# A fused sparse attention and gated FFN kernel: the first FFN unit of three blocks becomes two units of two blocks, fed by 1 KB reads on two DMA queues

## The chip, the cores and the metric

The kernel runs on one core of a Trainium2 chip. A core has five engines with a program each: TensorE (PE: matrix products and transposes into PSUM), VectorE (DVE), ScalarE (ACT), GpSimd (POOL) and SyncE (SP, which here issues DMAs only). They meet at semaphores. Sixteen DMA engines move data between device memory and the on-chip buffer. The metric is device time in microseconds (us) of one launch, the median of three runs.

## The reference

Inputs are q, k and v of shape (4 batches, 8 heads, 768 rows, 64) and three FFN matrices (512 x 1536, 512 x 1536, 1536 x 512), all float32. For each batch and head:

```python
k_min, k_max = min and max of k over chunks of 32 keys          # 24 chunks
ub = sum over d of max(q * k_min, q * k_max)                    # bound of each query on each chunk
top = the 6 chunks of largest ub among those not after the query's own chunk
scores = q @ k.T / 8, kept where the key's chunk is in top and the key is not after the query
attn_out = softmax(scores) @ v
```

The heads are then put side by side, x is (3072, 512), and

```python
out = ((1 / (1 + exp(-(x @ w_gate)))) * (x @ w_val)) @ w_out
```

The first 128 rows of a batch see at most four chunks, so no choice is needed there: they are plain causal attention on the batch's first 128 keys.

## The kernel before

The work is cut into blocks of 128 query rows, six a batch. Three blocks make a **unit** of 384 rows (L659), and a unit goes through two stages: attention of its blocks, then its FFN. There are eight units. A "first" block of a batch (rows 0 to 127) needs only a simple path, `first` (L805); the others need bounds, choice of chunks and masks (`prepare`, L1191: `keys_wide`, `queries_wide`, `choose`), then `attend` (L1047). Unit 0 is made of the first blocks of batches 0, 1 and 2; unit 1 of blocks 1 to 3 of batch 0; unit 2 of blocks 4 and 5 of batch 0 and the first block of batch 3; the rest go on in order.

`load_first` (L731) reads k, q and v of a first block on SP's queue: k and q in two DMAs each (heads 0 to 3, heads 4 to 7), rows of 64 floats, so runs of 256 B (L742), v in one (L737). `first` turns k and q with four f32 TensorE transposes each (L815: `kfT`, `qfT`), copies them to f16 (`kf16`, `qf16`), makes scores (L852), exponentials (L857, ACT), the causal mask (L859, POOL), products with v (L866, `pvf`), divides (L872, L874), turns the result (L881, `xpsf`) and copies it into the unit's x (`xTf`, L885). For batch 0 it also makes minima and maxima of chunks (L825) and the key buffer `hk` (L831).

`ffn` (L1131) runs 12 blocks of 128 hidden columns. For each, four matmuls make the gate product `g` and four the value product `v` (L1146, 128 x 384), ACT takes tanh (L1154), DVE multiplies (L1158, `hg`). Then for each of three row blocks 12 matmuls make the output `o` (L1168), ACT or DVE evicts it (`osb`) and SP stores it (L1180). All FFN products of a unit and of all units are in one order on TensorE (the key "ffn").

The weights come on POOL's queue, converted to f16 on the way, in nine DMAs of 1 MB of f32: three of gate and value columns each (L718, L719), three of output rows (L724). The first pair waits for batch 1's q (L1202), the others for the last causal mask of unit 0 (L1203 to L1208). `load_wide` (L747) reads unit 1's and unit 2's k and q, `load_v` (L771) the values, both on SP.

The order on each engine is not written by hand: every operation is given to a planner (`Plan`, L72) with the engines that can do it, its cost, what it reads and writes, its buffers and a priority. `walk` (L110) places operations one at a time on engines by start time and priority, within limits on buffers (L558), and gives one fixed order for each engine, in which the program is then emitted. The table NUDGES (L304) shifts priorities, and LANDS (L492) holds the planner's landing times of DMAs. So every engine executes in the planned order; what comes late on the chip holds up what stands behind it.

Before the first loads land, POOL and DVE make identities and masks. The eight `hkp` copies (L704) write the mask pattern into the two key buffers.

Of the kernel before, what the change touches and what calls it, by code (L numbers as in the profile page):

```python
# [9 lines left out]
F16 = mybir.dt.float16  # L10
AF = mybir.ActivationFunctionType
ALU = mybir.AluOpType
AX = mybir.AxisListType
# [7 lines left out]
SHARED = {128: (0.145, 0.95), 256: (0.173, 0.90), 512: (0.22, 0.83), 768: (0.29, 0.78), 2048: (0.5, 0.5)}  # L21
SENT, LANDED = {SP: 700, POOL: 2700}, 1100
# [12 lines left out]
class Op:  # L35
    def __init__(self, name, engines, emit, prio, dma, rows, port):
        self.name, self.engines, self.emit, self.prio, self.dma = name, engines, emit, prio, dma
        self.rows, self.port = rows, port
        self.deps = []
        self.bufs = []  # L40
        self.start = self.done = self.engine = None

# [29 lines left out]
class Plan:  # L72
# [37 lines left out]
    def walk(self, land, prio=None, script=None, slow=1.0):  # L110
# [3 lines left out]
        line = {SP: 0.0, POOL: 0.0}  # L114
# [105 lines left out]
        while avail:  # L220
            best = None
            at = {}
            for op in avail:
                r = room(op)
                if r == FAR:
                    continue
                for e in op.engines:
                    at[op, e] = max(r, inputs(op, e))
# [27 lines left out]
    def landings(self, out, slow=1.0):  # L256

        queues = {SP: [], POOL: []}
# [6 lines left out]
        while queues[SP] or queues[POOL]:  # L265
# [5 lines left out]
            if len(on) == 2:  # L271
# [21 lines left out]
    def order(self):  # L293

        nudge = {n: int(x) for n, x in (w.rsplit(":", 1) for w in NUDGES.split())}
        lands = {n: float(x) for n, x in (w.rsplit(":", 1) for w in LANDS.split())}
        prio = {op: op.prio + nudge.get(op.name, 0) * 0.01 for op in self.ops}
# [7 lines left out]
ident:370 epat0:-92 epat:-143 kcr0:-70 kcr1:88 hq0:-119 hq1:74 ap0:168 v10:48 hkp000:102 hkp001:162 hkp010:1  # L305
hkp011:-53 ap1:113 v11:43 hkp100:139 hkp101:127 hkp110:-301 hkp111:-12 ident16:15 kf0_0:-159 kf1_0:-55 qf0_0:-66
qf1_0:-51 vf_0:27 kf0_1:-30 kf1_1:-16 qf0_1:-8 qf1_1:65 vf_1:10 kf0_2:24 kf1_2:41 qf0_2:-23 qf1_2:-11 vf_2:54
k0_u1:-125 k1_u1:-15 k2_u1:-44 k3_u1:35 q0_u1:-10 q1_u1:29 q2_u1:-4 q3_u1:38 v_0_1:-51 v_0_2:-11 v_0_3:24 kfT_0:99
kf16_0:-28 kxf0:60 kxf1:201 kcr_f:18 hkf0:348 hkf1:-115 qfT_0:94 qf16_0:-40 v16_0_0:238 scf_0:-96 expf_0_0:-210
cmf_0_0:18 pvf_0_0:-76 rzf_0_0:194 xf_0_0:-87 xpsf_0_0:190 xTf_0_0:126 expf_0_1:-202 cmf_0_1:-55 pvf_0_1:108  # L310
rzf_0_1:77 xf_0_1:-247 xpsf_0_1:216 xTf_0_1:349 kfT_1:222 kf16_1:-105 qfT_1:-70 qf16_1:-58 vf1_1:10 vc_1:-234
scf_1:49 expf_1_0:-380 cmf_1_0:208 pvf_1_0:-84 rzf_1_0:273 xf_1_0:-212 xpsf_1_0:67 xTf_1_0:-358 expf_1_1:-13
cmf_1_1:373 pvf_1_1:-205 rzf_1_1:48 xf_1_1:-97 xpsf_1_1:-211 xTf_1_1:-218 kfT_2:17 kf16_2:-63 qfT_2:-262 qf16_2:-119
vf1_2:-47 vc_2:-401 scf_2:-119 expf_2_0:66 cmf_2_0:-66 pvf_2_0:255 rzf_2_0:-8 xf_2_0:219 xpsf_2_0:-211 xTf_2_0:202
expf_2_1:-179 cmf_2_1:-80 pvf_2_1:247 rzf_2_1:84 xf_2_1:169 xpsf_2_1:-154 xTf_2_1:59 wv0:48 wg1:-259 wv1:-69 wg2:-2
wv2:1 wo0:-37 wo1:-37 wo2:30 kn_u1_0:121 kT_u1_0:338 kx0_u1_0:215 kx1_u1_0:9 kt_u1_0:-348 hk0_u1_0:-32 hk1_u1_0:-121
kn_u1_1:299 kT_u1_1:179 kx0_u1_1:118 kx1_u1_1:7 kt_u1_1:23 hk0_u1_1:-212 hk1_u1_1:-168 kn_u1_2:314 kT_u1_2:32
kx0_u1_2:84 kx1_u1_2:86 kt_u1_2:100 hk0_u1_2:223 hk1_u1_2:90 kn_u1_3:176 kT_u1_3:-24 kx0_u1_3:385 kx1_u1_3:83
kt_u1_3:-167 hk0_u1_3:64 hk1_u1_3:138 kcr_u1:-25 qn_u1_0:-215 qT_u1_0:68 qf_u1_0:-35 qm_u1_0:223 hq0_u1_0:-426
hq1_u1_0:-4 qn_u1_1:-36 qT_u1_1:84 qf_u1_1:-93 qm_u1_1:3 hq0_u1_1:-255 hq1_u1_1:145 qn_u1_2:20 qT_u1_2:-117  # L320
qf_u1_2:86 qm_u1_2:-137 hq0_u1_2:-331 hq1_u1_2:-54 qn_u1_3:-137 qT_u1_3:-59 qf_u1_3:-21 qm_u1_3:-21 hq0_u1_3:-280
hq1_u1_3:74 ub_u1:37 ubn0_u1:-7 mx0_u1:-11 ap0_u1:130 ubn1_u1:222 ubm1_u1:87 mx1_u1:25 ap1_u1:-112 apt0_u1:-48
hqm0_u1_0:16 hqm0_u1_2:7 apt1_u1:155 hqm1_u1_0:-182 hqm1_u1_2:-99 v16_0_1:177 v16_0_2:318 v16_0_3:471 g_u0_0:36
tanh_u0_0:-46 v_u0_0:-424 hg_u0_0:-188 g_u0_1:-109 tanh_u0_1:-131 v_u0_1:-383 hg_u0_1:-86 g_u0_2:-132 tanh_u0_2:-104
v_u0_2:-243 hg_u0_2:-198 g_u0_3:-77 tanh_u0_3:106 v_u0_3:-80 hg_u0_3:87 g_u0_4:-317 tanh_u0_4:-279 v_u0_4:-282
hg_u0_4:86 g_u0_5:-64 tanh_u0_5:-125 v_u0_5:-235 hg_u0_5:-7 g_u0_6:-14 tanh_u0_6:-83 v_u0_6:-416 hg_u0_6:-27
g_u0_7:-132 tanh_u0_7:54 v_u0_7:-309 hg_u0_7:70 g_u0_8:67 tanh_u0_8:-18 v_u0_8:-445 hg_u0_8:131 g_u0_9:-48
tanh_u0_9:-449 v_u0_9:-447 hg_u0_9:-33 g_u0_10:-62 tanh_u0_10:118 v_u0_10:-430 hg_u0_10:90 g_u0_11:-149
tanh_u0_11:-38 v_u0_11:-294 hg_u0_11:-101 o0_u0_0:267 o1_u0_0:95 o2_u0_0:-2 osb_u0_0:-109 out_u0_0:104 o0_u0_1:371
o1_u0_1:146 o2_u0_1:27 osb_u0_1:34 out_u0_1:315 o0_u0_2:288 o1_u0_2:44 o2_u0_2:258 osb_u0_2:-41 out_u0_2:135  # L330
# [977 lines left out]
```

The softmax here doesn't subtract the row's maximum and nothing guards it: scores larger than these inputs give would overflow.

## Time and profile before

| what | value |
|---|---|
| median of three runs | 295.02 us (294.74 to 295.06) |
| profiled execution | 295.64 us |
| its span, first to last instruction | 293.9 us |
| TensorE busy | 278.2 us |
| mean granted TensorE clock | 0.988 |
| first product of unit 0's FFN starts | 21.61 us |
| first issue of a weight DMA | 10.14 us |

The profile is of one execution. Busy time of an engine leaves out its waits and the issuing of DMAs; PE spans of pipelined matmuls overlap, so the distance between starts is the better price of one. A group of lines in a timeline gives start, length, engine, line of the kernel, operation, output and input, count, and in brackets the idle time ahead of it and what ended it. DMA share is the mean busy share of the sixteen DMA engines; it can exceed 1 where packets of several transfers overlap.

### The profile page before, as it was taken

To read this page: it belongs to the slowest core of one execution; us is meant where nothing else is said; L and a number is where in the kernel's file an instruction comes from. 1 tells how busy PE (TensorE), PEld (TensorE's weight loads), DVE (VectorE), ACT (ScalarE), POOL (GpSimd) and SP (SyncE) were. 2 spreads that over 40 slices of the span, in tenths; PEclk is the share of its full clock that TensorE was granted. 3 is DMA by queue.
4 is the path that set the end of the run, shared out by engine and by line. 5 is a ranking of instruction groups with operands and counts; after the bars stand their busy time and mean duration, and the time that the engine had idled before them with its cause. 6 is when DMAs were issued, how large, how long until landed. Compare 5 with 4: busy or idle time off the path is not lost.

```text
span 293.9 us, 6954 instructions
## 1 busy us (share of the span) xinstructions
PE 278.2 (95%) x2656; PEld 176.7 (60%) x2656; DVE 189.2 (64%) x560; ACT 195.8 (67%) x398; POOL 92.5 (31%) x162
## 2 busy tenths in 40 slices
PE   2879998999989999999999999999999999999994
PEld 2645555767664566556666667676565557655651
DVE  8375883996999289999999899654134124432420
ACT  7674757977984879458889898886563466323321
POOL 6681314933652337013326954213000011000000
PEclk9977999999999999999999999999999999999999
DMA  7999999999967999399997300001100110011002
GB/s 165 218 249 216 197 197 235 220 146 166 184 100 90 203 188 184 67 215 152 142 210 145 111 3 3 0 2 39 71 2 1 50 60 0 2 38 71 0 15 95
DMA packets 123233, 32.69 MB, mean 111 GB/s; under 512 B 111424, under 2 KB 120128, under 8 KB 123200
## 3 DMA queue, kind: packets, MB, share of 16 engines
q1 hardware_dynamic: 118448, 27.53, 53.1%
q0 software_dynamic: 4752, 4.72, 9.5%
q8 instruction: 21, 0.34, 0.5%
q14 instruction: 12, 0.10, 0.1%
HBM read 30.67 MB, written 6.29 MB: 126 GB/s over the span
## 4 chain that ended last, share of the span: by engine, by line
PE 78%; DMA 10%; DVE 4%; SPq 2%; POOL 2%; ACT 1%; issue 1%; ACTq 0%; DVEq 0%
PE o_u L1168 20%; PE v_u L1146 18%; PE g_u L1146 18%; PE sc_u L1063 11%; DMA wo<-in_moe_w_out_dram 9%; PE pv_u L1096 6%; PE ube_u L1002 2%; SPq L742 2%; PE xps_u L1123 2%; DMA qf<-in_q_dram 1%; DVE qf_u L969 1%; DVE kcr L787 1%; DVE kt L953 1%; ACT attf L857 1%; PE qfT L815 1%
## 5 line engine op out<-in xcount | busy, mean ns | idle before, releaser
L1074 ACT ACTIVATE att_u<-sc_u 128x512 f16<-128x512 f32 (+3 forms) x184 | 88.0, 549 | 13.9 <-PE sc_u L1063 13.1
L1158 DVE SCALAR_TENSOR_TENSOR hg_u<-gate_u,v_u 128x384 f16<-128x384 f16 x96 | 51.8, 544 | 53.8 <-PE v_u L1146 37.0
L1146 PE MATMUL g_u<-xT_u,wg 128*128 128x384 f16 x384 | 79.3, 330 | 0.0
L1146 PE MATMUL v_u<-xT_u,wv 128*128 128x384 f16 x384 | 78.8, 328 | 0.3 <-DMA wv<-in_moe_w_val_dram 0.3
L1154 ACT ACTIVATE gate_u<-g_u 128x384 f16<-128x384 f32 x96 | 47.6, 495 | 39.1 <-DVE hg_u L1158 21.5
L1168 PE MATMUL o_u<-wo,hg_u 128*128 128x512 f16 x288 | 68.0, 379 | 1.1 <-DMA wo<-in_moe_w_out_dram 1.1
L1080 POOL TENSOR_SCALAR_AFFINE_SELECT att_u<-att_u 128x384 f16<-128x384 f16 (+1 forms) x56 | 28.4, 512 | 99.0 <-ACT att_u L1074 98.2
L1146 PEld LDWEIGHTS <-wv 128*128 128x128 f16 x384 | 36.8, 98 | 23.5 <-issue 0.8
L1146 PEld LDWEIGHTS <-wg 128*128 128x128 f16 x384 | 36.5, 99 | 21.8 <-issue 1.5
L1168 PEld LDWEIGHTS <-hg_u 128*128 128x128 f16 x288 | 27.1, 98 | 28.7 <-issue 1.5
L1177 ACT ACTIVATE osb_u<-o_u 128x512 f32<-128x512 f32 x20 | 12.1, 603 | 26.7 <-PE o_u L1168 25.0
L1096 PEld LDWEIGHTS <-att_u 128*128 128x128 f16 x640 | 25.5, 98 | 4.7
L1096 PE MATMUL pv_u<-v,att_u 128*128 128x65 f16 x640 | 28.0, 193 | 0.0
L1063 PE MATMUL sc_u<-hqo,hko 128*128 128x128 f16 (+2 forms) x220 | 27.8, 243 | 0.1
L1063 PE MATMUL sc_u<-hqe,hke 128*128 128x128 f16 (+2 forms) x220 | 27.1, 243 | 0.2 <-ACT att_u L1074 0.2
L1063 PEld LDWEIGHTS <-hke 128*128 128x128 f16 x220 | 16.8, 98 | 5.7 <-issue 1.2
L779 POOL CAST v<-v 128x512 f16<-128x512 f32 x23 | 13.9, 619 | 19.2 <-DMA v<-in_v_dram 18.9
L1063 PEld LDWEIGHTS <-hko 128*128 128x128 f16 x220 | 16.3, 98 | 4.8 <-issue 0.2
L576 DVE COPY xT_u<-xps_u 128x384 f16<-128x384 f16 (+1 forms) x17 | 5.7, 338 | 14.4 <-PE xps_u L1123 14.3
L1115 DVE TENSOR_TENSOR x_u<-pv_u,rz_u 128x384 f16<-128x384 f32 (+1 forms) x28 | 14.5, 523 | 0.4
L1025 DVE MAX8 mx_u<-ubn_u 128x8 f32<-128x8 f32 (+16 forms) x152 | 12.4, 156 | 0.1
L787 DVE TRANSPOSE_TENSOR_REDUCE kcr<-k 128x24 f32<-128x768 f32 x12 | 11.2, 941 | 0.8 <-DMA k<-in_k_dram 0.8
(119 smaller groups left out, 306.9 us busy)
## 6 DMA issues: line engine op xcount, KB each, us to landing
out_dram<-osb_u SPq DMA_DIRECT2D x24, 256.0 KB, 2.4
v<-in_v_dram SPq DMA_DIRECT2D x23, 256.0 KB, 5.0
k<-in_k_dram SPq DMA_DIRECT2D x12, 384.0 KB, 6.1
q<-in_q_dram SPq DMA_DIRECT2D x12, 384.0 KB, 6.8
wg<-in_moe_w_gate_dram POOLq DMA_DIRECT2D x3, 512.0 KB, 10.2
wv<-in_moe_w_val_dram POOLq DMA_DIRECT2D x3, 512.0 KB, 12.8
wo<-in_moe_w_out_dram POOLq DMA_DIRECT2D x3, 512.0 KB, 23.3
kf<-in_k_dram SPq DMA_DIRECT2D x8, 128.0 KB, 3.6
```

The source lines that it names most:

```text
L779: plan.add(f"v16_{b}_{ib}", {POOL: pool(H * D)}, lambda e: nc.gpsimd.tensor_copy(v16[b % 2][:, ib, :, 0:D], at(t)), reads=[t], writes=[("v ...
L787: plan.add(f"kx{m}_{name}_{p}", {DVE: dve(size)}, lambda e, m=m, op=op: nc.vector.tensor_reduce(out=outs[m](), in_=src(), op=op, axis=AX.X ...
L1025: nc.vector.max(at(mx)[:, e_, j, :], at(ubn)[:, e_, j, 0:max(8, u.seen[j])])
L1063: nc.tensor.matmul(at(t)[:, o:o + 128 * m], hk[b % 2][e_][:, p, 128 * jb:128 * jb + 128], hq[u.side][e_][:, p, 128 * x:128 * (x + m)], sta ...
L1074: plan.add(f"exp_{u.name}_{h}_{y}", {ACT: act(n)}, lambda e, t=t, att=att, b0=b0, n=n: nc.scalar.activation(at(att)[:, b0:b0 + n], at(t), ...
L1080: nc.gpsimd.affine_select(out=dv, in_=dv, compare_op=ALU.is_ge, fill=0.0, base=0, pattern=[[0, u.m], [1, 128]], channel_multiplier=-1)
L1096: nc.tensor.matmul(at(pv)[:, last, x, :], at(att)[:, c:c + 128], v16[b % 2][:, jb, h, :], start=(jb == 0), stop=(jb == ib))
L1115: plan.add(f"x_{u.name}_{p}", {DVE: dve(u.t)}, lambda e: nc.vector.tensor_tensor(at(x_).rearrange("p a (e d) -> p e a d", e=2), at(pv)[:, ...
L1146: nc.tensor.matmul(at(t), w16[:, c, 128 * fb:128 * fb + 128], at(u.xt)[:, c, :], start=(c == 0), stop=(c == 3))
L1154: plan.add(f"tanh_{u.name}_{fb}", {ACT: act(T)}, lambda e, g=g, gate=gate: nc.scalar.activation(at(gate), at(g), AF.Tanh, scale=0.5), read ...
L1158: plan.add(f"hg_{u.name}_{fb}", {DVE: dve(T)}, lambda e, w_=w_, gate=gate, hg=hg: nc.vector.scalar_tensor_tensor(at(hg), at(gate), 1.0, at ...
L1168: nc.tensor.matmul(at(o), at(hgs[fc])[:, 128 * tb:128 * tb + 128], wo16[:, fc, :], start=(fc == 0), stop=(fc == NFB - 1))
```

## The change

Unit 0 keeps the first blocks of batches 0 and 1 (256 rows). A new unit 8 has the first blocks of batches 2 and 3, and unit 2 is left with its two other blocks (256 rows). All sizes that were T = 384 in `ffn` follow the unit's rows. Unit 8's products form an order of their own ("ffn8") beside the others, and both small units make four gate products ahead of the first value product.

```diff
     units = [
-        Unit(0, [], [(0, 0), (1, 1), (2, 2)]),
+        Unit(0, [], [(0, 0), (1, 1)]),
         Unit(1, [(0, 1), (0, 2), (0, 3)]),
-        Unit(2, [(0, 4), (0, 5)], [(3, 2)]),
+        Unit(2, [(0, 4), (0, 5)]),
...
+        Unit(8, [], [(2, 0), (3, 1)]),
     ]
```

First blocks are read with four consecutive rows a partition (1 KB runs), k on SP's queue and q on ACT's; v alternates between the two. Since a partition then holds four rows, k and q are turned by eight f32 matmuls against the identity instead of four transposes, and the f16 copy puts the rows in order.

```diff
-                for e_ in range(2):
-                    plan.add(f"{n}f{e_}_{b}", {SP: (450, 450)}, lambda e, t=t[n], src=src, e_=e_: nc.sync.dma_start(
-                        at(t).rearrange("s (p e) d -> s e p d", e=2)[:, e_], heads(src, b, e_)[:, 0:128].rearrange("p s d -> s p d")),
...
+                for g in range(2):
+                    plan.add(f"{n}f{g}_{b}", {(SP, ACT)[j]: (450, 450)}, lambda e, view=view, src=src, g=g: issue(e).dma_start(
+                        view()[:, 256 * g:256 * g + 256], heads(src, b, g)[:, 0:128].rearrange("p (s r) d -> p s (r d)", r=4)),
...
             def turn(e, t=t, n=n):
-                for p in range(NP):
-                    nc.tensor.transpose(at(t)[:, p], at(raw[n])[:, 2 * p:2 * p + 2].rearrange("s e d -> s (e d)"), ident32)
...
+                for r in range(4):
+                    for g in range(2):
+                        c = 256 * g + 64 * r
+                        nc.tensor.matmul(at(t)[ROWS[g], r].rearrange("d p s -> d (p s)"), raw[n][0]()[:, c:c + 64], ident32,
+                                         start=True, stop=True)
```

The first pair of weight loads waits for batch 1's k. All weight loads are chained by the order of their issues, no longer by the last causal mask.

```diff
-    weights(0, -0.9, [(raw_f[1]["q"], 1)])
-    last = next(op for op in plan.ops if op.name == "cmf_2_1")
...
+    gate = [raw_f[1]["k"][1][1]]
+    weights(0, 4, -15.0, gate)
+    weights(4, 8, -1.6, [])
+    weights(8, 12, -1.6, [])
```

37 f32 matmuls of the identity with itself, whose result nobody reads, are put on TensorE: eight at the start, the others each not before a named step of a first block starts.

```diff
+    warm = ps("warm", "wm", [128, 128])
+    for name, n in {"": 8, "kfT_0": 2, "qfT_0": 3, "kfT_1": 3, "qfT_1": 3, "scf_1": 3, "kfT_2": 3, "qfT_2": 3, "scf_2": 3, "pvf_2_0": 3}.items():
+        for i in range(n):
+            op = plan.add(f"warm{name}_{i}", pe(213, 170), lambda e: nc.tensor.matmul(at(warm), ident32, ident32, start=True, stop=True),
+                          reads=["ident32"], writes=[warm], prio=5.0)
+            wake.append((op, name))
```

Buffers: the f16 keys, queries, values and attention weights of the first blocks are lent parts of batch 1's key and value buffers (and of `hq`) through a new class `Lent`; what writes those buffers later waits for the first blocks' last use. The bounds' transposed copy `ubn` shares the buffer of `qm`, whose next writer comes after it (`held`). There are three x buffers instead of two, 21 of `hg` instead of 18, and six of `np` instead of seven. The first four `hkp` copies come after unit 8's first gate product, the other four after unit 1's.

The planner knows a third queue (ACT) and a new table of packet prices, an operation can be given an earliest start (table HOLDS), and NUDGES and LANDS have new values throughout, so the order on every engine is planned anew.

## The prediction

> **What bounds the kernel now.** First the page: busy shares, then the strip of 40 slices (7.35 us each).
> ```profile
> PE 278.2 (95%) x2656; PEld 176.7 (60%) x2656; DVE 189.2 (64%) x560; ACT 195.8 (67%) x398; POOL 92.5 (31%) x162
> ...
> PE   2879998999989999999999999999999999999994
> ...
> PEclk9977999999999999999999999999999999999999
> DMA  7999999999967999399997300001100110011002
> ```
> TensorE is the bound almost everywhere, and only the first seven slices (to 51 us) show anything to recover: PE at 2, 8, 7, a clock of 7 tenths in slices 3 and 4, and DMA engines that are full from slice 2 on. So I cut the span into stretches (busy us of each engine, count, granted clock, DMA share, GB/s):
> ```profile
> 0.00:21.60 21.60, 12.61 (x93) 9.16 (x94) 14.08 (x38) 15.21 (x25) 14.97 (x30) 0.93 1.09 210
> 21.60:48.10 26.50, 25.05 (x178) 14.44 (x176) 17.70 (x60) 16.68 (x39) 6.62 (x13) 0.93 1.19 211
> 48.10:62.40 14.30, 13.99 (x189) 9.88 (x190) 12.46 (x43) 11.86 (x32) 8.81 (x20) 1.00 1.00 202
> 62.40:289.00 226.60, 225.53 (x2199) 142.97 (x2200) 144.94 (x422) 151.50 (x304) 62.07 (x101) 1.00 0.51 85
> ```
> From 48.1 us PE is idle 0.31 + 1.07 us in 241 us. Whatever makes the kernel faster must get more TensorE work done before 48 us or remove such work. The waits of PE before 65 us (us in total, times, longest) and its timeline where the first products start say how the early time goes:
> ```profile
> PE kfT L815 <- DMA kf<-in_k_dram: 5.9, 2, 5.0
> PE pvf L866 <- POOL attf L859: 1.2, 2, 1.1
> PE o_u L1168 <- DMA wo<-in_moe_w_out_dram: 1.1, 1, 1.1
> ```
> ```profile
> 19.82 0.42 PE L881 MATMUL xpsf<-ident,xf 128*128 128x128 f16 x2
> 20.91 0.90 PE L901 MATMUL kT_u<-ident,kn_u 128*128 128x128 f32 x3 [0.67 <-ACT kn_u L574]
> 21.61 1.49 PE L1146 MATMUL g_u<-xT_u,wg 128*128 128x384 f16 x4
> 22.89 1.49 PE L1146 MATMUL v_u<-xT_u,wv 128*128 128x384 f16 x4
> 24.17 1.38 PE L1146 MATMUL g_u<-xT_u,wg 128*128 128x384 f16 x4
> 25.39 0.81 PE L1146 MATMUL v_u<-xT_u,wv 128*128 128x384 f16 x4
> 26.04 0.81 PE L1146 MATMUL g_u<-xT_u,wg 128*128 128x384 f16 x4
> ```
> Start to start a product of four matmuls is 1.28 us at first, 0.65 us from 25.39 on: three products lose 0.63 + 0.63 + 0.57 = 1.83 us to the halved clock. And the products cannot start before 20.6 us, since the third block's x is turned only at 19.82 (copied out at 20.28 + 0.29). Last, the chain that ended last runs through the weight stream, not through PE:
> ```profile
> 7.48 3.85 DMA qf<-in_q_dram
> ...
> 22.11 25.94 DMA wo<-in_moe_w_out_dram
> 48.09 1.89 PE o_u L1168 x8
> ```
> The weights land (issue time plus time to landing) at 18.3, 22.2, 27.3, 31.2, 34.6, 38.0, 41.4, 44.7 and 48.05 us, 3.7 us apart on average; PE filled nearly all of that time with other work.
>
> **What the Trainium skill says.** "TensorE: Matmul & The Clock Gate", Part 1: the array runs at 1.2 GHz until about 3.4 us of activity and at 2.4 GHz after. The trace agrees: 1.28 against 0.65 us. "DMA: Bandwidth & Descriptors", Specifications: runs under 512 B fall below line rate; same page, Issuing engines are not separate DMA queues: a second queue only saves issue time. The trace agrees as far as it goes: SP issues one load per 0.55 us and the engines move 124 GB/s in the first 5 us, 210 afterwards with 256 B runs; no 1 KB run is in it. "TensorEngine Tiling (Array Packing)", Restrictions: column tiling switches the fast FP32 transpose off. The trace has both forms: a turned block of four is 0.44 to 0.47 us (60.17, 60.64, 61.08), and the column-tiled f32 bounds (L1002, 320 columns, eight tiles side by side) take 36.47 to 37.03, so 0.56 us, 0.22 us for 128 columns.
>
> **The ledger before.** I count useful TensorE work at full-clock prices. One first block costs, in the saturated stretch where the block of batch 3 runs, 0.47 + 0.44 (turns) + 0.33 (scores) + 0.14 + 0.13 (values) + 0.23 (x turned) = 1.74 us. Up to 21.6: three blocks 5.2, three key turns of unit 1 at 0.33, so 6.2 us. From 21.6 to 48.1: 26.5 - 1.45 idle - 1.83 cold = 23.2. Done by 48.1: 29.4 us.
>
> **The change, part by part.**
> (1) *Loads.* Twelve k and q loads of batches 0 to 2 go from 256 B to 1 KB runs, four for batch 3 come forward from 50.9 us, with its v. At 210 GB/s 128 KB took 0.6 us. The 1 KB price is not shown: no gain 0.6, at best the page's fabric ceiling 0.3; I take 0.4. Sixteen at 0.4 plus a v of 1.2 instead of twelve at 0.6 is 7.6 against 7.2 us: no DMA time is saved before 48 us, it is only used sooner. SP and ACT issue together, so k and q of batches 0 and 1 (1 MB) land at about 6.2 us (first issue 0.81, 1.4 us to data, 4 us of transfer), where batch 1's q came at 10.1. A load moved to ACT occupies it for about 0.5 us: ten of them, 5 us, take the place of two 1.47 us constant copies (3.09, 4.58), which move.
> (2) *Weights* are gated by batch 1's k instead of its q: first issue 10.14 to about 6.3. They then share with 2 MB of first blocks still to come, so I give half of it back: 2 us earlier, first gate weights at 16.5, last output weights at 46 (at most 3.8, at least 0).
> (3) *Turns.* Eight turns of plain f32 matmuls in place of eight transposes. Four pairs at 0.22 us are 0.9 if the two column halves run side by side (as L1002's tiles do), 1.8 if not; I take 1.0. The extra 0.55 x 8 = 4.4 us lies in the first 17 us, where PE was idle for 9 us of 21.6, so it costs nothing; without that cover it is 2.2 us for the two blocks ahead of the first product.
> (4) *Two units of 256 rows.* Unit 0 needs two blocks only. Batch 1's x is ready 7 us after its q in the trace (qfT 10.18 to xT 16.80 + 0.37); 6.2 + 7 + 2 x 0.55 and 1 us of ACT issue gives about 15.3. So the first product starts with the weights, S = 17 (15.5 to 21). Unit 8 follows about 6 us later. Split products: 384 columns are 162.5 ns, 128 are 55, so 256 are 109; three units of 24 x 4 x 109 = 31.4 against two at 31.2: +0.2 us. Evictions: 36 at about 0.37 (ACT) and 0.42 (DVE) against 24 at 0.49 and 0.54: +1.6 and +2.2 us, mostly at 21.6 to 48.1 us, where ACT has 9.8 and DVE 8.8 us free, and batch 3's own evictions leave 55 to 69 us; 0.
> (5) *Batch 3's block* leaves the saturated stretch; in the ledger it counts as work done early.
> (6) *Warming matmuls*, 37 f32 ones of 0.22 us: ahead of S in idle time they cost nothing and save the 1.83 us of cold clock. Those after S stand in PE's fixed order ahead of real products; some five in the way: 1.1 us (0 to 3).
> (7) *Moved constants and shared buffers.* Eight mask copies (0.5 us each on DVE) leave 3 to 8 us: four come after unit 8's first product, four after unit 1's, at 64 to 80 us, where DVE is 85% and ACT 98% busy and PE waited 0.8 us for DVE once: 0.3 us (0 to 1.5). The bounds' transposed copy sharing the queries' buffer makes the next unit's positive part wait; before, the copies were read by 40.9 and the next queries come at 50: 0. The borrowed key and value buffers are free long before batch 1's keys: 0.
>
> **The sum.** By S = 17 two blocks (3.5) and the turns of the other two (1.8) are done: 5.3. From 17 to 48.1 are 31.1 us, less 1.1 for (6) and 0.3 of cold clock, less waits. Waits: between gate and value weights (3.5 us apart) only 1.7 us of gate products and some 0.6 of block work are ready: 1.2 idle. To the second gate weights 5 us hold 1.7 of value products, 3.5 of unit 8 if its x is there by 23, and 1.4 of other work: about 1. Later each quarter brings 7 us of products per 7 us of stream and the last output wait of 1.12 us goes. Scattered waits, as many as before: 1. So 5.3 + 31.1 - 1.1 - 0.3 - 3.2 = 31.8 us done against 29.4: 2.4 us gained. After 48.1 (4) and (7) take some 0.4. Net 2.0. The tail (last eviction and store, 4 us) is unchanged. What is late next is the weight stream: it sets S and the 3.2 us of waits.
> The profiled execution is 295.64 us (span 293.9 and 1.74 around it): 293.6 after. The median shown is 0.62 lower, 295.02: so **293.0 us**.
>
> **Rivals.** *A, the stream only moves the wait* (0.16): the DMA engines are already full, the extra batch and the earlier start cancel, S is 19 to 20 and PE waits in 20 to 36 us. Against it: PE has unit 8's 7 us of products in hand. Gain 2.0 - 2.5 + 0.5 of smaller waits: 295.0.
> *B, ACT as an issuer is late* (0.16). ACT runs in order; behind its ten loads are the casts of k and q, the exponentials and x copies of the four blocks, and PE waits for each. SP's issues of first blocks rose from 0.5 to 0.99 us when its queue was backed up (5.86): ten such are 10 us instead of 5. It decides when unit 0's x comes later than the first value weights (about 20 us). At S = 21.5 the 2.4 us of gain lose 4.5, get back 2.0 of the waits for weights (landed by then), lose 0.8 to a late x of unit 8 and the 0.4 after 48 us: 1.3 us slower than before, 296.3; with a cold start too, 297.5.
> *C, more than that* (0.08): weights 3.8 us earlier, S = 15.5, no waits after 25: 290.7.
> That the change does nothing is excluded: a third of the early products change size and place.
>
> **Chances.** The forecast has 0.60, with its own range 291.4 to 294.4. 0.2% (0.6 us) is about what a measurement of this kernel can tell from no change. Faster: nearly all of 0.60, C, and a little of A: 0.67. Same: 0.11 (most of A). Slower: 0.22 (B and the bad end of A). Range for 8 in 10: 291.0 to 296.6.
>
> **What would show it.** Right: first product near 17 us with PEclk full to 26 us; unit 8's products by 24; first wg issue near 6.3; no wait for wo; no kfT or qfT after 24 us; PE idle under 2 us after 48. Wrong: ACT's issues over 0.8 us, S beyond 20, turns at 1.8 us, or DVE the releaser of PE at 64 to 85 us.

## The result, and the profile after

The changed kernel takes 317.14 us (median; 316.12 to 317.45) where the kernel before takes 295.04 (294.74 to 295.08): a ratio of 1.0746 [1.0720, 1.0771]. The prediction said 293.0 us, with 291.0 to 296.6 around it. It was wrong in sign and by more than ten times the size. An execution more than 1.5% above the fastest of its kernel counts as slow and is left out of every ratio below; this concerns two of the seven executions of one version, the hold on batch 1's queries.

Beside the strip shown of before, these are the same rows of the page after (40 slices of 7.88 us):
```profile
PE 289.3 (92%) x2916; PEld 199.9 (63%) x2916; DVE 193.9 (61%) x574; ACT 191.7 (61%) x401; POOL 100.2 (32%) x169
...
PE   4242799999999999999999999999999999999995
...
ACT  0002677749879783879489678977767663363321
...
PEclk9555599999999999999999999999999999999999
DMA  2935899995984999997890089201100010001002
```
All of the loss is in the first five slices. PE is idle for most of 30 us, ACT does nothing at all before the fourth slice, and the DMA engines, which were full from the second slice on before, are at 3 and 5 tenths in slices 3 and 4. From the sixth slice on PE is as full as ever. The cut into stretches says when (busy us of each engine, granted clock, DMA share, GB/s):
```profile
0.00:5.00 5.00, 3.41 (x16) 3.22 (x16) 2.38 (x8) 0.00 (x0) 3.22 (x13) 1.00 0.13 37
...
15.00:20.00 5.00, 1.97 (x16) 1.57 (x16) 0.00 (x0) 0.00 (x0) 0.00 (x0) 0.50 0.53 120
20.00:25.00 5.00, 1.98 (x16) 1.58 (x16) 0.00 (x0) 0.00 (x0) 0.00 (x0) 0.50 0.42 102
25.00:30.00 5.00, 1.22 (x12) 1.22 (x14) 0.00 (x0) 0.32 (x1) 0.00 (x0) 0.50 0.33 97
```
In the first 5 us, when hardly anything but the first blocks' loads is under way (the first weights are issued at 4.83 us), they move 37 GB/s; the kernel before moved 124. And while loads are what everyone waits for, at 20 to 30 us, the DMA engines are more than half idle. A path that is waited for and is not full is the finding to follow. PE's waits to 65 us, its timeline at the turns and the first products, and the chain that ended last:
```profile
PE qfT L894 <- DMA qf<-in_q_dram: 8.7, 2, 5.1
PE kfT L894 <- DMA kqvf<-in_k_dram: 4.9, 1, 4.9
PE kfT L894 <- DMA kf<-in_k_dram: 4.0, 2, 2.1
PE scf L934 <- DVE hke L633: 2.8, 1, 2.8
```
```profile
16.33 1.97 PE L894 MATMUL qfT<-ident,qf 128*64 128x128 f32 x16 [5.11 <-DMA qf<-in_q_dram]
21.94 1.98 PE L894 MATMUL qfT<-ident,qf 128*64 128x128 f32 x16 [3.64 <-DMA qf<-in_q_dram]
28.78 1.98 PE L894 MATMUL kfT<-ident,kqvf 128*64 128x128 f32 x16 [4.86 <-DMA kqvf<-in_k_dram]
...
44.58 1.91 PE L1232 MATMUL g_u<-xT_u,wg 128*128 128x256 f16 x16
```
```profile
0.81 1.16 ACTq L819
2.00 8.67 DMA qf<-in_q_dram
10.69 18.57 DMA kqvf<-in_q_dram
29.68 1.28 ACT L631
```
Loads of 128 KB hold the chain for 27 us. The queries of batches 0 and 1 are awaited until 21.94 us, where the prediction had them landed at 6.2, and the first product starts at 44.58 instead of 21.61. Last, ACT's own timeline:
```profile
0.81 3.74 ACTq L819 DMA_DIRECT2D qf<-in_q_dram  x4
5.30 12.56 ACTq L819 DMA_DIRECT2D kqvf<-in_q_dram  x3
21.92 1.29 ACTq L814 DMA_DIRECT2D vf<-in_v_dram  x1
27.07 0.55 ACTq L819 DMA_DIRECT2D kqvf<-in_q_dram  x1
29.28 0.37 ACTq L814 DMA_DIRECT2D kqvf<-in_v_dram  x1
29.68 1.28 ACT L631 ACT_TABLE_LOAD   x1 [29.68 <-DMA kqvf<-in_q_dram]
```
ACT's first computing instruction comes at 29.68 us, behind its tenth load. So two causes offer themselves: the loads are slow (few DMA engines), or ACT as an issuer is late (rival B). They can't be told apart by looking, since each would delay the other.

### The profile page after: what moved, and what is told of

Same layout as the page of the kernel before. It is cut to its first block, busy times and chain, and to the rows that moved or that the text cites. A ratio compares the mean times of both kernels' runs of the same rounds, so it can differ in the third digit from the quotient of the medians.

```text
span 315.2 us, 7516 instructions
## 1 busy us (share of the span) xinstructions
PE 289.3 (92%) x2916; PEld 199.9 (63%) x2916; DVE 193.9 (61%) x574; ACT 191.7 (61%) x401; POOL 100.2 (32%) x169
## 4 chain that ended last, share of the span: by engine, by line
PE 85%; DMA 9%; DVE 3%; ACT 1%; issue 1%; ACTq 0%; DVEq 0%
PE g_u L1232 19%; PE v_u L1232 19%; PE o_u L1271 19%; PE sc_u L1152 11%; PE pv_u L1185 6%; DMA kqvf<-in_q_dram 6%; DMA qf<-in_q_dram 3%; PE ube_u L1091 3%; PE warm L1302 2%; PE xps_u L1212 2%; PE kfT L894 1%; PE qfT L894 1%; PE kT_u L984 1%; PE qT_u L984 1%; PE scf L934 1%
## 5 line engine op out<-in xcount | busy, mean ns | idle before, releaser
L1163 ACT ACTIVATE att_u<-sc_u 128x512 f16<-128x512 f32 (+3 forms) x184 | 89.2, 547 | 16.2 <-PE sc_u L1152 15.9
L1232 PE MATMUL v_u<-xT_u,wv 128*128 128x384 f16 (+1 forms) x432 | 79.5, 308 | 0.0
L1232 PE MATMUL g_u<-xT_u,wg 128*128 128x384 f16 (+1 forms) x432 | 79.4, 308 | 0.0
L1252 DVE SCALAR_TENSOR_TENSOR hg_u<-gate_u,v_u 128x384 f16<-128x384 f16 (+1 forms) x108 | 53.0, 499 | 42.8 <-PE v_u L1232 34.7
L1245 ACT ACTIVATE gate_u<-g_u 128x384 f16<-128x384 f32 (+1 forms) x108 | 49.0, 457 | 40.3 <-PE g_u L1232 22.8
L1271 PE MATMUL o_u<-wo,hg_u 128*128 128x512 f16 x288 | 68.8, 379 | 0.0
L1169 POOL TENSOR_SCALAR_AFFINE_SELECT att_u<-att_u 128x384 f16<-128x384 f16 (+1 forms) x56 | 29.5, 533 | 114.1 <-ACT att_u L1163 113.8
L1232 PEld LDWEIGHTS <-wg 128*128 128x128 f16 x432 | 40.9, 98 | 19.1 <-issue 1.2
L1232 PEld LDWEIGHTS <-wv 128*128 128x128 f16 x432 | 41.1, 98 | 18.0
L1302 PE MATMUL warm<-ident 128*128 128x128 f32 x68 | 12.3, 311 | 1.4 <-POOL ident masks.py:199 1.4
```

Of the source, the lines that this page charges most:

```text
L1163: plan.add(f"exp_{u.name}_{h}_{y}", {ACT: act(n)}, lambda e, t=t, att=att, b0=b0, n=n: nc.scalar.activation(at(att)[:, b0:b0 + n], at(t), ...
L1169: nc.gpsimd.affine_select(out=dv, in_=dv, compare_op=ALU.is_ge, fill=0.0, base=0, pattern=[[0, u.m], [1, 128]], channel_multiplier=-1)
L1232: nc.tensor.matmul(at(t), w16[:, c, 128 * fb:128 * fb + 128], at(u.xt)[:, c, :], start=(c == 0), stop=(c == 3))
L1245: plan.add(f"tanh_{u.name}_{fb}", {ACT: act(u.rows)}, lambda e: nc.scalar.activation(at(gate), at(g), AF.Tanh, scale=0.5), reads=[g], writ ...
L1252: plan.add(f"hg_{u.name}_{fb}", {DVE: dve(u.rows)}, lambda e: nc.vector.scalar_tensor_tensor(at(hg), at(gate), 1.0, at(w_), ALU.add, ALU.m ...
L1271: nc.tensor.matmul(at(o), at(hgs[fc])[:, 128 * tb:128 * tb + 128], wo16[:, fc, :], start=(fc == 0), stop=(fc == NFB - 1))
```

## The experiments

**Slow loads or a late issuer?** The Trainium skill, "DMA: Bandwidth & Descriptors", section "Why a DMA increments its semaphore by 16 and not by 1", says that a DMA uses as many engines as the largest number up to 16 that divides the slowest dimension, of length over 1, of both its access patterns. The change's source pattern is "p (s r) d -> p s (r d)": its slowest dimension is the four heads, so four engines. The packet counts of the page fit. This is ACT's queue after (packets, MB, share):
```profile
q10 hardware_dynamic: 3136, 1.57, 1.8%
```
Eight loads of 128 runs of 1 KB are 1,024 packets, two of 1,024 runs of 256 B are 2,048; 64 are left, packets of 4 bytes in the trace, and those are the completions: 8 x 4 + 2 x 16. With sixteen engines each they would be 160. Theory E puts the loss on this engine count, A on ACT as the issuer, R on the rest of the change. The first edit puts the rows of the block, not its heads, first in the source pattern; the runs are still 1 KB, and the matmuls that turn it and the copies read the other order:

```diff
-  view()[:, 256 * g:256 * g + 256], heads(src, b, g)[:, 0:128].rearrange("p (s r) d -> p s (r d)", r=4)),
+  view()[:, 256 * g:256 * g + 256], heads(src, b, g)[:, 0:128].rearrange("p (s r) d -> s p (r d)", r=4)),
```

> The changed kernel with one thing altered: the k and q loads of first blocks walk rows first and heads second, so that the slowest dimension of the source is 32 and no longer 4 (same bytes, same 1 KB runs, same two queues, same order on all engines; the turned columns are sorted accordingly). Theory E (a load whose source starts with a dimension of 4 is spread over 4 of the 16 DMA engines only): loads land by 8 us, first product near 17 us, 291 to 295 us. Theory A (ACT as an issuer blocks, rival B of the prediction): nothing changes for ACT's queue, 312 to 318 us. Theory R (1 KB runs or the f32 turns are slow in themselves): 310 to 318 us.

303.42 us (300.81 to 305.05), ratio 1.0261 [1.0189, 1.0333]: 14 of the 22 us are back, 8 are not. Its first product starts at 30.97 us, not near 17. ACT's queue now has the 160 completions:
```profile
q10 hardware_dynamic: 3232, 1.57, 1.9%
```
The share counts the time of the packets: 91 us in sum for the same bytes in the change, 93 us here. So the packets on four engines were no slower; fewer of them ran at once. The complement of this edit leaves the four heads first and takes ACT out:

```diff
-        return nc.scalar if e == ACT else nc.sync
+        return nc.sync
```

> The changed kernel with all loads of first blocks issued by SP, in the planned order, and none by ACT; still a first source dimension of 4. Theory E: 16 loads of 32 packets on each of the same 4 engines at about 50 ns are at least 26 us, so 308 to 318 us, no better than 3 to 8 us under the change. Theory A: ACT is free, 292 to 297 us.

316.2 us (one run): without ACT as an issuer the change is as slow, so A alone is not it. Then the same pair of patterns in the kernel before, which has one queue and none of the rest of the change. Its transposes then find other rows in each place, so the first blocks' attention is not the reference's in these two.

```diff
-  at(t).rearrange("s (p e) d -> s e p d", e=2)[:, e_], heads(src, b, e_)[:, 0:128].rearrange("p s d -> s p d")),
+  at(t).rearrange("s h d -> s (h d)")[:, 256 * e_:256 * e_ + 256], heads(src, b, e_)[:, 0:128].rearrange("p (s r) d -> p s (r d)", r=4)),
```

> The kernel before, with its 16 k and q loads of first blocks as 1 KB runs with heads (4) as the slowest source dimension, all on SP; the rows reach other places of the tile, so the attention of the first blocks is not the reference's. No ACT queue, no new turns, no new units. Theory E: the 12 early loads take 1.6 to 2.2 us each instead of 0.6, 12 to 19 us later, less some cover: 303 to 314 us. Theory A and theory R's turns: 293 to 296 us.

312.43 us (one run), 17 more than before, from one access pattern. With the rows first in the same place:

```diff
-  heads(src, b, e_)[:, 0:128].rearrange("p (s r) d -> p s (r d)", r=4)),
+  heads(src, b, e_)[:, 0:128].rearrange("p (s r) d -> s p (r d)", r=4)),
```

> As before_narrow, but rows (32) as the slowest source dimension: 1 KB runs over all 16 engines, one queue; the attention of the first blocks is not the reference's either. Theory E: 12 loads at about 0.4 instead of 0.6 us, last q up to 2 us earlier, weights gated by batch 1's q earlier: 292.5 to 295.2 us. Theory R (1 KB runs slow): 300 us or more.

295.84 us (294.66 to 297.24), ratio 1.0023 [1.0005, 1.0040]. So E holds in both kernels: in the kernel before, the two orders of the same 1 KB runs are 17 us apart. The runs by themselves gain nothing here. They do take less of the DMA engines: the hardware queue's share of the page falls from 53.1% to 50.5%. But in the first 5 us, with one load issued per 0.55 to 0.65 us, the DMA engines are not full in either (0.55 and 0.37; 124 and 107 GB/s), and the first product starts no sooner (23.14 us against 21.61).

**What holds the other 8 us.** In the version with the spread loads (rows first, sixteen engines) POOL issues weights at 4.83 us, in the kernel before at 10.14. The prediction had counted on a gate; on the chip there is none. That the first weights "wait" for batch 1's q, or now its k, as the descriptions of the kernel and of the change put it, is a dependence in the planner's model alone: it sets the order on each engine, and no semaphore goes with it, as the weights overwrite nothing. Before, the loads stood on POOL behind a cast of v (9.58 us), which did wait. POOL and two loads of the version with spread loads (the second view has KB each and us from issue to landing):
```profile
4.83 0.92 POOL L782 DMA_DIRECT2D wg<-in_moe_w_gate_dram  x1
5.74 0.75 POOL L782 DMA_DIRECT2D wv<-in_moe_w_val_dram  x1
6.48 0.75 POOL L782 DMA_DIRECT2D wg<-in_moe_w_gate_dram  x1
19.60 0.61 POOL L917 CAST v<-vf 128x512 f16<-128x512 f32 x1 [12.37 <-DMA vf<-in_v_dram]
```
```profile
kqvf<-in_k_dram SPq DMA_DIRECT2D x4, 128.0 KB, 10.3
...
vf<-in_v_dram SPq DMA_DIRECT2D x1, 256.0 KB, 13.5
```
Three megabytes of weights go out between 4.8 and 7.2 us; the small loads issued after that take 7 to 16 us by kind, and the first value rows hold POOL until 19.6. The same skill page, section "Queues, rings and completion order", says that an engine takes packets in turn from the queues that have work; that fits a large transfer slowing small ones behind it, but no run here shows the packets' turns.

Two edits, each alone and together (theory P: the weights let go too soon; W: ACT waits for its own loads). ACT keeps only the queries of batches 0 and 1, the other six loads (two of them values, in the same way) go to SP:

```diff
-  plan.add(f"{n}f{g}_{b}", ..., lambda e, view=view, src=src, g=g: issue(e).dma_start(
+  plan.add(f"{n}f{g}_{b}", ..., lambda e, view=view, src=src, g=g: (issue(e) if b < 2 else nc.sync).dma_start(
```

And a real hold: a copy of two columns of batch 3's queries on POOL, ahead of the first weights:

```diff
+            def load(e, t=t, src=src, n=n):
+                if n == "wg" and lo == 0:
+                    nc.gpsimd.tensor_copy(gate_t, raw_f[3]["q"][0]()[:, 0:512:511])
+                nc.gpsimd.dma_start(t[:, :, 128 * lo:128 * hi], src[:, :, 128 * lo:128 * hi])
```

> The spread kernel (303.4 us) with ACT issuing only the four q loads of batches 0 and 1, which wait for nothing; the other six of its loads go to SP in the planned order. All other orders unchanged. Theory W (what is left is ACT standing still until 13.0 us, because its fifth to tenth load each wait for a landing eight loads earlier): the first scores come at 9 instead of 16.9 us, 295 to 298 us. Theory P (three weight loads start at 4.83 us, before the first blocks are read, and the small runs of v and the last q crawl beside them): the values of batch 0 and the last q still land at 19 to 23 us, 300 to 304 us.

303.06 us, ratio 1.0237 [1.0181, 1.0294]: nothing. ACT computes from 3.70 us on, but the first scores come at 16.73 us, not 9: PE waits 6.4 us for keys instead (3.4 with ten loads on ACT), caught behind the weights. A last version of this kind, with the spread loads all on SP (the edit of the complement above):

> The spread kernel with all loads of first blocks on SP. W is gone as in spread_act4, and the second queue with it: q of batches 0 and 1 lands up to 2 us later. Theory W: 296 to 299 us. Theory P: 301 to 306 us.

301.06 us (one run), as P said.

> The spread kernel with one POOL copy of two columns of batch 3's q ahead of the first weight load, so that the weights really wait for the last q (about 9 to 10 us; the planner's gate is no wait on the chip). ACT's ten loads stay. Theory P: v of batch 0 lands by 12 us and the last q by 10, 296 to 299 us. Theory W: ACT still stands until its last issue; 300 to 304 us.

298.16 us (296.73 to 299.24), ratio 1.0090 [1.0067, 1.0114]: 5 of the 8 us. The profile of the held version shows the weights at 13.50 us and the same two kinds of load landing in 4.4 us for 10.3 and 5.1 for 13.5:
```profile
13.37 0.18 POOL L785 COPY gate_t<-kqvf 128x2 f32<-128x2 f32 x1 [8.46 <-DMA kqvf<-in_q_dram]
13.50 0.92 POOL L786 DMA_DIRECT2D wg<-in_moe_w_gate_dram  x1
```
```profile
kqvf<-in_k_dram SPq DMA_DIRECT2D x4, 128.0 KB, 4.4
...
vf<-in_v_dram SPq DMA_DIRECT2D x1, 256.0 KB, 5.1
```

> Both edits. If W and P are all that is left: first product at 17 to 19 us, 292 to 295 us. If neither matters, 300 to 304 us.

299.46 us, ratio 1.0123 [1.0076, 1.0170]: not the 292 to 295. With sixteen of the twenty loads of first blocks on SP the hold ends later (14.36 us for 13.37), and on POOL the cast of v and the first masks stand behind it. PE's first line of waits in this version:
```profile
PE pvf L954 <- POOL attf L947: 5.6, 1, 5.6
```

**The warming matmuls.** The change and the forecast speak of 37; the numbers in the diff add up to 34, and the profile has 68 records of them, two each. In the held version 18 stand ahead of the first product, eight at the start and ten between 21.2 us and the first product, and 16 after it. (The expectations below say 20 of 37 and 29 for 18 of 34 and 26.) This version drops all but the first eight, the order otherwise kept:

```diff
     for op in plan.order():
-        op.emit(op.engine)
+        if not op.name.startswith("warm") or op.name[4] == "_":
+            op.emit(op.engine)
```

> The spread loads with weights held until batch 3's queries have landed, and of the 37 warming matmuls only the first eight; the other 29 stay in the plan's order but are not issued. Theory M (the later warming matmuls stand in PE's way): in the same kernel with all 37 they took some 2.6 us of PE between 21.2 us and its first product (24.85) and 3 us or more up to 40 us, so 292.5 to 295 us against 298.2. Rival Q (they only fill waits for weights or evictions that then show themselves): 297 to 298.5. Rival K (without them the clock falls back): 298 to 300, with a granted clock under 0.9 somewhere after 20 us.

> The same without any warming matmul. The first eight run from 1.4 to 5.0 us, ahead of the first load's landing. If they are worth something, it is an earlier full clock for the turns of the first two blocks: 0.5 to 1.5 us slower than with the eight. If nothing turns on them: within 0.4 us of it.

> The spread loads with weights held on batch 3's queries, keeping the warming matmuls that stand ahead of the first product in PE's order (20 of 37). With all 37 the first sixteen matmuls of products took 1.91 us, at the full clock, from 24.85 us; with only eight, 3.25 us from 23.47. If the early ones pay for themselves and the late ones cost (theory M): 295 to 296.4 us, under the version with eight. If what the early ones give back is what they take: 296.4 to 297.2, the same as with eight. If the late ones only fill waits: 297.5 to 298.5, as with all.

With eight 296.65 us (ratio 1.0028 [1.0015, 1.0042]), with none 297.16 (1.0048 [1.0030, 1.0065]), with the 18 ahead of the first product 297.61 (1.0088 [1.0072, 1.0103]), with all 298.16 (1.0090). So the 16 after the first product cost nothing that can be told (theory M fails in its place), and the ten just ahead of it cost about 1.8 us, 0.6% by the ratios. The first product with all, with eight and with none (the line of each version's timeline):
```profile
24.85 1.91 PE L1237 MATMUL g_u<-xT_u,wg 128*128 128x256 f16 x16
```
```profile
23.47 3.25 PE L1237 MATMUL g_u<-xT_u,wg 128*128 128x256 f16 x16 [0.20 <-DVE xT_u L633]
```
```profile
25.19 1.91 PE L1237 MATMUL g_u<-xT_u,wg 128*128 128x256 f16 x16 [0.20 <-DVE xT_u L633]
```
With eight it starts 1.38 us sooner than with all and takes 1.34 longer, at the halved clock: in these two profiles the trade is even for the first gate products. But that the ten are what keeps the clock full is not shown: with no warming matmul at all the first product ran at the full clock, and with eight and an earlier hold on the weights it did too (below, 23.92 us). Each is the profile of one execution. The value products start at 26.52 us with eight instead of 27.23, where the version with all waits 0.47 us for their weights; where the rest of the difference comes from the profiles don't say. The eight at the very start are worth nothing that can be told: 1.0028 and 1.0048 have intervals that overlap.

In the change as it was made:

> The change as it was made, with only the first eight warming matmuls. Until its first product at 44.6 us PE waits for loads, so most of the 29 others lie in idle time: 0 to 1.5 us faster than the 317.1 us of the change if the clock holds; up to 3 us faster if those after 44.6 us count in full; slower by 0.5 to 2 if the first products then run at half clock.

314.43 us, ratio 1.0656 [1.0638, 1.0674]: 2.7 us, 0.9% of the time, at the top of what was expected. The clock held: the first product starts at 43.45 us and takes 1.91.

**When may the weights go?** Three points on one trade: a hold on batch 2's queries with ACT's loads reduced to four, without and with the reduced warming, and a version where the hold, on batch 3's queries, stands behind the cast of v and a mask:

> The spread loads, ACT issuing only the queries of batches 0 and 1, and the weights held on batch 2's queries instead of batch 3's (so from about 9.5 us instead of 14.4, where the cast of batch 0's values and the masks stood behind the hold on POOL and PE waited 5.6 us for a mask). Theory W (with the weights out of the way, ACT's wait for its own loads is what is left of the delay before the first product): first product at 20 to 22.5 us and 294.5 to 297 us. Rival V (the small loads of batch 3 and the values are caught behind the weights again): first product at 24 or later and 298 to 302 us.

305.34 us, ratio 1.0315 [1.0273, 1.0356], worse than either forecast. ACT is free early, but SP, with sixteen loads, issues the values of batches 2 and 3 only at 11.2 to 13.6 us, and the weights have been going since 9.46. PE's first two waits in it:
```profile
PE pvf L954 <- POOL hko L635: 4.6, 1, 4.6
PE qfT L899 <- DMA kqvf<-in_q_dram: 3.1, 1, 3.1
```
POOL's cast (hko) waited for these values until 31.49 us.

> Both: ACT with four loads, weights held on batch 2's queries, and only the first eight warming matmuls. If W and M both hold and add up: first product at 18 to 20.5 us and 290 to 293 us, faster than the kernel before. If only one of them holds: 294 to 297. If neither: 298 or more.

303.34 us, ratio 1.0243 [1.0209, 1.0277]: neither sum came out. Dropping the warming matmuls gave 2 us; the loads stay caught.

The third version puts the held loads behind the cast and the mask on POOL:

```diff
+    ops = plan.order()
+    back = [named[n] for n in ("wg0", "wv0", "wg4")]
+    for op in back:
+        ops.remove(op)
+    at_ = ops.index(named["cmf_0_1"]) + 1
+    ops[at_:at_] = back
```

> The spread loads, ACT issuing only the queries of batches 0 and 1, the first eight warming matmuls, weights held on batch 3's queries; on POOL the held loads stand behind the cast of batch 0's values and the first mask, so PE no longer waits for that mask (5.6 us before). If the ACT issues and this mask are what is left of the loss: no wait for the mask, first product at 23.5 to 24.5 us when the first weights land, more of the four first blocks done by then, 293 to 295.5 us. If the weights' late start is what is left (they land from some 24 us on where the kernel before has them at 18.3): 296 to 298, as with the version where ACT issues ten loads.

297.93 us, ratio 1.0095 [1.0071, 1.0119]. The wait for the mask is gone, and the first product waits for weights instead, and runs cold:
```profile
24.70 3.59 PE L1237 MATMUL g_u<-xT_u,wg 128*128 128x256 f16 x16 [1.25 <-DMA wg<-in_moe_w_gate_dram]
```
So a hold until everything has landed is too late and, with a slow issuer, an early one catches the last loads. Between them, with ACT issuing its ten loads (so that all loads of first blocks are out by 10 us) and eight warming matmuls:

```diff
-                    nc.gpsimd.tensor_copy(gate_t, raw_f[3]["q"][0]()[:, 0:512:511])
+                    nc.gpsimd.tensor_copy(gate_t, raw_f[2]["q"][0]()[:, 0:512:511])
```

> The version with eight warming matmuls and ACT as an issuer of ten loads, its weights held on batch 2's queries instead of batch 3's (13.4 us): when all loads of the first blocks but two of batch 3 and its values are issued. If the weights' late landing (22.3 us for the first, 18.3 in the kernel before) is what is left: weights issued 2 us or more earlier, first product at 20.5 to 22.5 us, 294 to 295.8 us against 296.7. If the last small loads are caught behind the weights, as they were where ACT issued only four: first product no earlier than 24 us, or PE waiting for batch 3's values or queries after it, 297 to 304.

295.15 us (294.63 to 296.19), ratio 1.0004 [0.9986, 1.0021]: the time of the kernel before. The first product, at the full clock, is still at 23.92 us, not the 20.5 to 22.5 expected:
```profile
23.92 1.91 PE L1237 MATMUL g_u<-xT_u,wg 128*128 128x256 f16 x16 [0.20 <-DVE xT_u L633]
```
PE waits 4.4 us for casts, and ACT begins to compute at 9.95 us only, behind its own loads.

> The same with the hold on batch 1's queries, where the plan itself has it. If the small loads still to be issued then are caught: PE waits for the queries or keys of batches 2 and 3, as without a hold, and 298.5 to 303 us. If not: 293 to 295.5 us, and the hold that the plan counts on is the right one.

296.73 us (296.35 to 301.73), ratio 1.0059 [1.0030, 1.0088]: slower than with batch 2's. Five of the seven executions took 296.4 to 298.5 us, between the two forecasts; whether small loads are caught is not shown for them.

Last, with the hold on batch 2's queries, half of batch 3's queries and its values go from ACT to SP:

```diff
-  lambda e, view=view, src=src: issue(e).dma_start(
+  lambda e, view=view, src=src: (nc.sync if b == 3 else issue(e)).dma_start(
...
-  lambda e, view=view, src=src, g=g: issue(e).dma_start(
+  lambda e, view=view, src=src, g=g: (nc.sync if (b, g) == (3, 0) else issue(e)).dma_start(
```

> The version with the hold on batch 2's queries, with the last two of ACT's ten loads (half of batch 3's queries, batch 3's values) on SP. In it ACT began its first cast only at 9.95 us, behind those two, and PE waited 4.4 us for what follows from it. If this wait is what is left: ACT begins at about 7.9 us, PE's wait is 2 us or more shorter, first product at 21.5 to 22.5 us, 292.5 to 294.5 us, faster than the kernel before. If the weights (19.2 and 23.1 us) take the wait over, or batch 3's two loads, now issued up to 2 us later, are caught behind them: 294.8 to 299 us.

294.14 us (292.68 to 296.24), ratio 0.9973 [0.9955, 0.9991]: 0.8 us under the kernel before, by an interval that just leaves out no change. It has the best time of sixteen versions of the change, and the best of many tries looks better than it is. Its first product and its first waits (the profiled execution took 296.23 us, one of its longest, with a mean clock of 1.000):
```profile
20.19 1.91 PE L1237 MATMUL g_u<-xT_u,wg 128*128 128x256 f16 x16 [0.20 <-DVE xT_u L633]
```
```profile
PE pvf L954 <- POOL hko L635: 1.7, 1, 1.7
PE scf L939 <- DVE hke L633: 1.6, 1, 1.6
```
PE's wait for the casts went from 4.4 to 1.6 us and the first product came 3.7 us sooner. Of these, 1.7 are the earlier first scores (12.12 us for 13.80). The other 2.0 lie between first scores and first product (8.07 us for 10.12), where this execution had the full clock: two turns took 1.09 and 1.04 us, and 1.97 and 1.92 in the profile with ten loads on ACT; that the shorter wait is what kept the clock up is not shown. Only 1 us of the 3.7 is in the time: from 20 to 52 us PE is busy 27.1 of 32 us, in the version with ten loads on ACT 30.1 (8.79 + 9.43 + 11.91). Part of it is seen as a wait for a cast of values: those of batches 2 and 3 are again caught behind the weights (10.8 us from issue to landing, 5.9 in the version held on batch 3's queries). And the last wo weights still land at 48.06 us.

| version | ratio to before | step, % of the time |
|---|---|---|
| the change | 1.0746 | |
| 16 engines | 1.0261 | -4.9 |
| weights held on batch 3's queries | 1.0090 | -1.7 |
| eight warming matmuls | 1.0028 | -0.6 |
| held on batch 2's queries | 1.0004 | -0.2 |
| two of ACT's loads to SP | 0.9973 | -0.3 |

The first two steps are far outside the noise, and the third is clear of it (1.0090 [1.0067, 1.0114] against 1.0028 [1.0015, 1.0042]). In each of the last two the intervals overlap, so neither alone is shown. The steps are taken in this order; in another they differ (the warming matmuls are 0.9% in the change itself, ACT's loads nothing that can be told as long as the weights are not held). The order on the engines is the planned one throughout, apart from what the edits move; what a new plan with the real landings would give was not tried.

## Why the prediction was wrong, point by point

**(1) Loads: the step that failed.** "The 1 KB price is not shown: no gain 0.6, at best the page's fabric ceiling 0.3; I take 0.4." The bounds of the unknown price looked only at the run length, and took it for granted that a load keeps its sixteen engines: a term that the step put at nothing without a reason. The diff shows the other thing that changed: the slowest dimension of the source pattern, from 128 rows to 4 heads. With four engines instead of sixteen that is 4.9% of the time here and 17 us in the kernel before. "k and q of batches 0 and 1 (1 MB) land at about 6.2 us" became 21.94; with sixteen engines these eight loads had landed at 7.2 to 7.6 us (the held version and those built on it), near the prediction. The price of the run length itself, 0.4 against 0.6, was harmless.

**(1), the other half: ACT as an issuer.** "Ten of them, 5 us" priced the issues, which took 0.37 to 1.73 us each. It left out that an issue can wait. In the trace the loads of SP and ACT raise eight semaphores in turn, and each later load first waits for the semaphore that it will raise, that is, until the load eight before it has landed: ACT's fifth load waits for the semaphore of its first, the sixth for that of its second. For SP the profile lists such waits:
```profile
SPq L819 <- DMA kf<-in_k_dram: 8.8, 3, 4.0
SPq L814 <- DMA kf<-in_k_dram: 3.9, 1, 3.9
```
So ACT, which runs in order, does no arithmetic until its tenth load is away: 29.68 us in the change, 13.02 with sixteen engines, 9.95 to 10.20 with the weights held as well. Rival B had the sign and the engine ("behind its ten loads are the casts of k and q"), at 1.3 to 2.5 us. The wait is real; taking two loads from ACT was worth 0.3% at best once the other two are out of the way, within the noise of that step; taking all ten from it in the change gave nothing that its one run can tell (316.2 us).

**(2) Weights.** "Gated by batch 1's k instead of its q: first issue 10.14 to about 6.3." It was 4.83, and no gate: the dependence is one of the planner's. The step read a dependence in the code as a wait on the chip; the timeline before showed what really held the weights, the cast at 9.58 us on POOL. Without a hold the first weights did land early, at 15.46 us in the change and 14.45 with the spread loads (16.5 predicted), but the small loads behind them came too late to use it. With a hold that let most small loads through nothing was left: the version that beats the kernel before has its first weights at 18.36 us and its last at 48.06, where that one has 18.3 and 48.05. No version had the 2 us of earlier weights and the small loads in time as well.

**(3) Turns.** The price was right: 0.93 to 1.02 us each at the full clock (1.0 predicted), 1.75 to 1.90 at the half clock. That the extra time lies in idle time was only half right: the last four turns stand on the way from the first scores to the first product, where PE has no idle time (33.53 to 44.58 us in the change, two of the four at the half clock).

**(4) Two units.** The split products cost 0.435 us for four, as 4 x 109 ns said. S = 17 failed through (1) and (2): 44.58 us. In the best version it is 20.19, with a last wait for DVE's copy of x (0.20 us); its first weights had landed at 18.36.

**(5), (7) and the end.** No wait for wo in the change, no DVE or POOL releaser of note later: from 48 to 62.4 us PE is busy all the time, from 62.4 to 310 us 247.41 of 247.6 us. This part of the prediction held, though with everything else late the change tests it only weakly; in the best version PE is busy 225.04 of 225.6 us from 62.4 to 288. (The busy shares that (7) gives for 64 to 80 us, DVE 85% and ACT 98%, are those of 70 to 80 us; over the whole stretch they are 82% and 89%.)

**(6) Warming.** 1.1 us (0 to 3) predicted, for those that stand after the first product; 2.7 us in the change and 1.5 in the held version, within the range. That is luck: in the held version those after it cost nothing that can be told, and those ahead of it, which were to be free, do. And there are 34, not 37.

**The rivals.** None of the three doubted that the stream of loads runs full. The first 5 us of the profile after refute it at once (0.13 at 37 GB/s), but the profile of before could not show it; it had to be read from the access pattern. The forecast's net gain of 2.0 us is not reached either: in the best version here, with the three defects reduced, the two units of two blocks gain 0.8 us (0.3 to 1.3 by its interval), and what PE does sooner it mostly loses again in waits between 20 and 52 us. Whether the plan itself is worth more, in an order made for these landings, stays open.

## What to carry to other kernels

When a diff turns an access pattern around, price the number of engines that share the load before the length of its runs: read the slowest dimension of both sides (17 us here for 4 in place of 32). Look, for every gate that a plan claims, for the instruction on the chip that waits; if none does, large transfers can start ahead of small ones and the small ones pay (13.5 us to landing for 5.1 here). And for an engine that issues loads and computes, look for what its issues wait for: ACT's first arithmetic came at 29.68 us in the change.

## What was not expected of the hardware

- The same bytes in the same 1 KB runs took 312.4 or 295.8 us of kernel time depending only on the order of the source's dimensions.
- Runs of 1 KB in place of 256 B took less of the DMA engines (50.5% for 53.1%) and no less time (1.0023).
- Loads of 256 KB in 256 B runs landed 5.1 us after their issue without weights in flight, and 13.5 us with 3 MB of them.
- Leaving out ten warming matmuls ahead of the first product gained about 0.6% of the time, although the one profile shows a cold start with them gone (1.38 us sooner, 1.34 us longer); without any warming matmul the profiled first product ran at the full clock.
